# Coarse attention and MoE in one kernel: group-pair loads, a fixed list for the lead-in, and v rows used directly in half of the first coarse output

## The chip, the core and the metric

One core of one Trainium2 chip. The metric is the time of one execution in microseconds (us) on the device, as a median over runs. A core has a matrix engine (TensorE, PE in the profile), a vector engine (VectorE, DVE), an activation engine (ScalarE, ACT), a general engine (GpSimd, POOL), a queue engine (SyncE, SP) and 16 DMA engines. All of them run their own list of instructions in order and wait for one another by semaphores. PSUM is the accumulator memory that matrix products are written to.

## What is computed

q, k and v have 4 batches, 8 heads, 576 positions and 64 columns. Attention is the sum of a coarse part (means over groups of 4 positions, 144 groups) and a local part (a band of 7 positions). Its output, as 2304 tokens x 512, goes through a mixture of 8 experts (512 to 1024 to 512) that are all computed and weighted by a gate with 8 normalizing rounds.

```python
q_d = q.reshape(B, H, Sd, factor, D).mean(axis=3)      # the same for k_d, v_d; factor = 4
out_d = sm_attn(q_d, k_d, v_d)
out_up = np.repeat(out_d, factor, axis=2)
mask = np.abs(pos[:, None] - pos[None, :]) < factor
out_local = np.matmul(softmax(where(mask, scale * q @ k.T, -1e9)), v)
x = (out_up + out_local) as tokens x 512
P = exp(logits - logits.max())          # logits = x @ w_gate
for _ in range(8): normalize P over experts, then over tokens
for e in range(E):
    out += P[:, e:e + 1] * (np.maximum(x @ w1[e], 0.0) @ w2[e])
```

## The kernel before

**Tokens and experts.** The groups are cut into six chunks: three of 64 groups (256 tokens) and three of 128 groups (512 tokens). The expert products begin when chunk 0 is ready: experts 0 to 2 are run on chunk 0 alone, in 24 units of one 128-wide slice of the hidden size each, then experts 3 to 6 on chunks 0 and 1, and so on. Each fp32 matrix is split into a high and a low part, and each product is three matmuls (high by high, high by low, low by high). A unit is 12 matmuls `psh` (L1167, 256 columns), ACT's `hh` (L1224), DVE's `hl` (L1227) and 6 matmuls `psy` of 512 columns (L1195 to L1197). Weights come as raw 256 KB tiles `r`; ACT makes `w1h`, `w2h` (L251, later L1287), POOL or DVE `w1l`, `w2l` (L253, later L1310 on POOL and L1306 on DVE).

**Attention.** For each unit of the local part (`l_gen`) DVE and POOL make products (L357), DVE sums them to scores (L381), masks and normalizes them (L396 to L417), DVE and POOL make products with v (L431) and DVE sums them to `lo` (L462). From b = 1 on the coarse part comes from sums written to memory. For the first 64 groups of b = 0 it is made by functions of their own, in the lead-in, in two halves of four heads, hf0 and hf1, from raw rows `dr` which `d_load` brings: `first_k` sums k over its groups with matmuls against an identity (`pssum`, L654) and ACT copies it to `kz` (L660); `first_v` does that for v (`psv`, L676, to `dv`, L681); `first_q` for q (`psq`, L628); `first_d` makes scores (`pss`, L695), maxima on DVE (`nm`, L705), exponentials on ACT (L708), sums (`sm`, L714), transposes (`pst`, L726), copies (`pt`, L736) and the coarse output (`pso`, L747, to `od`, L755). `x_gen` then puts `lo` in order (`psx`, L942), adds `od` (L948) and splits the sum into `xhs` (ACT, L955) and `xls` (DVE, L958). A third piece, `d_gen`, computes coarse rows 64 to 143 of b = 0 (`psd` L781, `qz` L790, `pss` L840, `st` L848, exponentials L852, transposes `psd` L873, `pt` L878); it borrows one PSUM bank, `psd`, that the local part of the next chunk also uses for its scores (L417 writes it, L431 reads it).

**What sets the order.** Every step is written as a generator ("thread") which gives the engine it wants next and an estimated time from which it can run. In the lead-in (until chunk 0 of x is ready) a loop picks the thread with the earliest estimated time. After that a planner, `sched`, picks the step that can start first by its estimated clocks, ties going by a table of ranks (`RANK`). Engines execute in the order in which the planner has written the instructions, so its estimates fix each queue.

Of the kernel before, what the change touches and what calls it, by code (L numbers as in the profile page):

```python
# [20 lines left out]
def attention_moe_kernel(  # L21
# [597 lines left out]
    v_set = {}  # L619
# [22 lines left out]
    def first_k(hf, kz):  # L642

        for p in range(2):
# [4 lines left out]
            rv = raw[0:HK].rearrange("p k h (a d) -> p k h a d", a=R)  # L649
            ps = y_tile([128, 2, HK], "pssum")  # L650
            for kh in range(2):
                for r in range(R):
                    for h in range(2):
                        nc.tensor.matmul(  # L654
                            out=ps[64 * h:64 * h + 64, kh], lhsT=rv[:, kh, h, r, :], rhs=ident[0:HK, 0:HK],
                            start=(r == 0), stop=(r == R - 1),
                        )
# [6 lines left out]
    def first_v(hf):  # L664

        t_sb = ap2.tile([Q1, 2, 4, D], F32, tag="dv", name="dv")
        done = 0.0
        for p in range(2):
            while (0, hf, p, 2) not in d_raw:
                yield None  # L670
            raw, t_raw = d_raw.pop((0, hf, p, 2))
            yield t_raw
            rv = raw[0:HK].rearrange("p k h (a d) -> p (k h) a d", a=R)
            ps = y_tile([HK, 4, D], "psv")
            for r in range(R):
# [3 lines left out]
            t = pe(3.4, t_raw)  # L679
            yield t + HOP  # L680
            nc.scalar.activation(  # L681
                out=t_sb[0:HK, :, 2 * p:2 * p + 2, :], in_=ps.rearrange("p (k h) d -> p k h d", k=2), func=AF.Copy
            )
            done = act(256, t)
        d_sum[0, hf, 2] = (t_sb, done)

    def first_d(hf, qf):

        while not qf_set or hf not in k_set:
# [11 lines left out]
        sme = su2.tile([128, 2, 2], F32, tag="sme", name="sme")  # L701
        sm = su2.tile([128, 2], F32, tag="sm", name="sm")
        pp = su2.tile([128, 2, SD], F32, tag="pp", name="pp")
        nc.vector.memset(sme, EPS)
# [33 lines left out]
        while (0, hf, 2) not in d_sum:  # L738
            yield None
        vs, t_v = d_sum.pop((0, hf, 2))  # L740
        v_set[hf] = vs
        yield max(t, t_v) + HOP
        ps = ps_h.tile([128, 2, Q0], F32, tag="h", name="pso")
        for p in range(2):
            for i in range(2):
                for kh in range(2):
                    nc.tensor.matmul(  # L747
                        out=ps[64 * i:64 * i + 64, p], lhsT=vs[0:HK, kh, 2 * p + i, :], rhs=pt[:, p, kh, i],
                        start=(kh == 0), stop=(kh == 1),
                    )  # L750
        t = pe(1.4, t, t_v)
# [667 lines left out]
    with tc.manual_schedule():  # L1419
# [74 lines left out]
        def first_x(aa):  # L1494
            for a in aa:
                yield from x_gen(0, a)

# [19 lines left out]
        th["x"] = Thread(first_x((0, 1)))  # L1517
        eng = {"l": "dve", "p": "pool"}
# [610 lines left out]
```

## Time and profile before

| | us |
|---|---|
| median of 3 runs | 1657.15 |
| lowest and highest run | 1655.9 and 1658.35 |
| profiled execution | 1658.6 |
| its span in the trace | 1656.8 |
| mean granted TensorE clock in it | 0.984 |

The page gives busy time of each engine over the span. The rows further down are from the timeline (start, duration, what an instruction writes and reads, how many are merged in a row, and in brackets how long the engine had been idle before and what ended that) and from a table of windows (busy time of each engine in a stretch, the clock that was granted to TensorE, where 0.50 is 1.2 GHz and 1.00 is 2.4 GHz, and what the DMA engines moved). fp32 matmuls that are not split leave two records each, so 16 matmuls are 32 records.

### The profile page before, as it was taken

Reading aid. Unit: us, or ns where it says so; the run is one execution under the profiler, and the core shown is the slowest. Engines: PE = TensorE matmul, PEld = TensorE weight load, DVE = VectorE, ACT = ScalarE, POOL = GpSimd, SP = SyncE. Lnnn points to the kernel's source line nnn. Section 1 sums busy time; section 2 is a strip of 40 time slices with the busy share of each in tenths; the row PEclk is TensorE's granted clock in tenths of the full one; section 3 lists DMA queues with packets and bytes.
Section 4 is the critical chain, followed back from the end, with each engine's and each line's share of the span. In section 5 each row is a group of like instructions: output and inputs, shape, how many; then the busy total and the mean of one; then the engine's idle time right before and its main releaser. Section 6 shows DMA issues by size and latency. Waiting matters only on the chain.

```text
span 1656.8 us, 21885 instructions
## 1 busy us (share of the span) xinstructions
PE 1623.1 (98%) x7845; PEld 1341.0 (81%) x7845; DVE 1007.6 (61%) x1244; ACT 639.3 (39%) x1300; POOL 907.0 (55%) x806
## 2 busy tenths in 40 slices
PE   7999999999999999999999999999999999999998
PEld 5878887888887787887888888888888888888887
DVE  6988889955888759477544464444444444444444
ACT  2654554454454343233333243333333333333331
POOL 5787645586566464566544266444444444444441
PEclk6899999999999999999999999999999999999999
DMA  9689666676664355434221233111111111111112
GB/s 196 168 220 213 176 150 166 161 211 188 167 162 148 114 183 168 139 115 135 76 60 55 95 113 91 52 53 54 53 51 51 51 51 51 51 52 51 52 38 51
DMA packets 201833, 183.68 MB, mean 111 GB/s; under 512 B 23676, under 2 KB 150780, under 8 KB 201468
## 3 DMA queue, kind: packets, MB, share of 16 engines
q1 hardware_dynamic: 194011, 168.65, 37.8%
q10 hardware_dynamic: 7712, 13.64, 2.6%
q8 instruction: 61, 1.00, 0.3%
q14 instruction: 49, 0.39, 0.1%
HBM read 161.66 MB, written 20.58 MB: 110 GB/s over the span
## 4 chain that ended last, share of the span: by engine, by line
PE 88%; DVE 6%; DMA 3%; issue 1%; ACT 1%; POOL 1%; SPq 0%; ACTq 0%; POOLq 0%; DVEq 0%
PE psm L1908 25%; PE psh L1167 15%; PE psy L1988 9%; PE psy L1989 9%; PE psy L1990 9%; PE psy L1195 5%; PE psy L1197 5%; PE psy L1196 5%; PE psh L1388 1%; DVE lo L462 1%; DMA r<-in_moe_w_dram 1%; DVE bsum L1698 1%; DVE prod L431 1%; PE pss L840 1%; DVE tl L1698 1%
## 5 line engine op out<-in xcount | busy, mean ns | idle before, releaser
L1765 POOL TENSOR_TENSOR w2l<-r,w2h 128x512 fp32r<-128x512 f32 x88 | 113.9, 1294 | 377.9 <-ACT w2h L1764 373.9
L1664 DVE SCALAR_TENSOR_TENSOR acc<-psy,lg,acc 128x512 f32<-128x512 f32 x176 | 131.4, 750 | 251.1 <-PE psy L1990 247.5
L1310 POOL TENSOR_TENSOR w1l<-r,w1h 128x512 fp32r<-128x512 f32 x128 | 170.9, 1335 | 159.4 <-ACT w1h L1287 137.3
L1731 POOL TENSOR_TENSOR c1l<-r,c1h 128x512 fp32r<-128x512 f32 (+1 forms) x176 | 206.0, 1196 | 51.7 <-ACT c1h L1728 51.0
L1310 POOL TENSOR_TENSOR w2l<-r,w2h 128x512 fp32r<-128x512 f32 x132 | 179.4, 1360 | 46.0 <-ACT w2h L1287 39.5
L1728 ACT ACTIVATE c1h<-r 128x512 fp32r<-128x512 f32 (+1 forms) x176 | 89.2, 567 | 242.5 <-POOL r L1736 242.5
L1195 PE MATMUL psy<-w2h,hh 128*128 128x512 f32 x416 | 169.1, 406 | 1.8 <-ACT sp L1263 1.6
L1197 PE MATMUL psy<-w2h,hl 128*128 128x512 f32 x416 | 163.5, 393 | 1.8 <-DVE hl L1227 1.8
L1196 PE MATMUL psy<-w2l,hh 128*128 128x512 f32 x416 | 163.5, 393 | 0.0
L1990 PE MATMUL psy<-w2h,xl 128*128 128x512 f32 x400 | 155.6, 389 | 0.0
L1227 DVE SCALAR_TENSOR_TENSOR hl<-psh,hh 128x512 fp32r<-128x512 f32 (+1 forms) x136 | 76.3, 561 | 102.6 <-ACT hh L1224 102.2
L1908 PE MATMUL psm<-tl,c1h 128*128 128x512 f32 x352 | 137.9, 392 | 0.0
L1908 PE MATMUL psm<-th,c1l 128*128 128x512 f32 x352 | 137.9, 392 | 0.0
L1908 PE MATMUL psm<-th,c1h 128*128 128x512 f32 x352 | 137.9, 392 | 0.0
L1988 PE MATMUL psy<-w2h,xh 128*128 128x512 f32 x352 | 136.9, 389 | 0.0
L1989 PE MATMUL psy<-w2l,xh 128*128 128x512 f32 x352 | 136.9, 389 | 0.0
L1167 PE MATMUL psh<-xhs,w1l 128*128 128x256 f32 (+1 forms) x384 | 123.9, 323 | 4.0 <-DVE w1l L1306 4.0
L1167 PE MATMUL psh<-xhs,w1h 128*128 128x256 f32 (+1 forms) x384 | 126.7, 330 | 0.0
L1224 ACT ACTIVATE hh<-psh 128x512 fp32r<-128x512 f32 (+1 forms) x136 | 67.2, 494 | 152.9 <-PE psh L1167 152.5
L1167 PE MATMUL psh<-xls,w1h 128*128 128x256 f32 (+1 forms) x384 | 123.5, 322 | 0.0
L462 DVE TENSOR_REDUCE lo<-prod 128x256 f32<-128x1792 f32 x36 | 121.8, 3392 | 0.3
L1988 PE MATMUL psy<-w2h,xhs 128*128 128x512 f32 x304 | 118.5, 390 | 0.6 <-DVE acc L1664 0.6
(221 smaller groups left out, 3862.1 us busy)
## 6 DMA issues: line engine op xcount, KB each, us to landing
r<-in_moe_w_dram SPq DMA_DIRECT2D x464, 256.0 KB
spill<-sp ACTq DMA_DIRECT2D x42, 256.0 KB
s<-spill SPq DMA_DIRECT2D x42, 256.0 KB
sums<-dr SPq DMA_DIRECT2D x36, 64.0 KB
out_dram<-acc ACTq DMA_DIRECT2D x16, 128.0 KB
lw<-in_k_dram SPq DMA_DIRECT2D x5, 336.0 KB
lw<-in_v_dram SPq DMA_DIRECT2D x5, 336.0 KB
lw<-in_v_dram SPq DMA_DIRECT2D x7, 224.0 KB
```

Of the source, the lines that this page charges most:

```text
L462: nc.vector.tensor_reduce(out=ot[:, :, h % 2], in_=pr.rearrange("p r w d -> p r d w"), axis=AX.X, op=ALU.add,)
L1167: nc.tensor.matmul(out=ps, lhsT=w[:, kk], rhs=x[:, kk], start=(kk == 0 and j == 0), stop=(kk == 3 and j == 2),)
L1195: nc.tensor.matmul(out=ye[z], lhsT=hh[:, ts], rhs=h2, start=(f2 == 0), stop=False)
L1196: nc.tensor.matmul(out=ye[z], lhsT=hh[:, ts], rhs=l2, start=False, stop=False)
L1197: nc.tensor.matmul(out=ye[z], lhsT=hl[:, ts], rhs=h2, start=False, stop=(f2 == NF - 1))
L1310: nc.gpsimd.tensor_tensor(out=l, in0=r, in1=h.bitcast(F32), op=ALU.subtract)
L1664: nc.vector.scalar_tensor_tensor(out=a, in0=y, scalar=g, in1=a, op0=ALU.mult, op1=ALU.add)
L1731: nc.gpsimd.tensor_tensor(out=ls[i][:, s], in0=r[:, s], in1=hs[i][:, s].bitcast(F32), op=ALU.subtract)
L1908: nc.tensor.matmul(out=ps, lhsT=wt[:, kk], rhs=xt[:, kk], start=start and j == 0, stop=j == len(seq) - 1, skip_group_check=not start,)
L1988: nc.tensor.matmul(out=y, lhsT=at_t(h), rhs=h2, start=(f == 0), stop=False)
L1989: nc.tensor.matmul(out=y, lhsT=at_t(h), rhs=l2, start=False, stop=False)
L1990: nc.tensor.matmul(out=y, lhsT=at_t(l), rhs=h2, start=False, stop=(f == 3))
```

## The change

**Loads.** The first k and v rows are read with two neighbouring groups in one partition (64 and 8 partitions x 2 heads x 512 values) where it was one group per partition in two halves (72 partitions x 2 heads x 256 values). The number of DMAs (8 for k, 8 for v) and the bytes are the same; the views in `first_k` and `first_v` follow.

**v rows directly.** For hf1 the group sums of v are no longer made ahead of the coarse output. `pso` sums over the raw rows instead: 32 matmuls from `dr` in place of 8 from `dv`. The summed v that `d_gen` needs later is made by four DVE reductions, after the coarse output is done. Two of four `psv` groups (8 of 16 matmuls) and two of four ACT copies go.

**Order.** The loop of the lead-in gives way to a list, `steps`. x of chunk 0 is two threads, x0 and x1, and `d_gen` starts within the lead-in. The memsets of `sme` stand first. In `sched` a short DVE step which has waited over 2 us for the port shared with POOL gets a better rank.

PE's instructions in the lead-in, up to the first coarse scores of the remaining rows and the first expert product: before,

```order
L628 MATMUL psq<-ident,lq 64x128 x16
L654 MATMUL pssum<-ident,dr 64x72 x64
L695 MATMUL pss<-kz_107,qf 128x144 x2
L676 MATMUL psv<-dr,ident 72x256 x4
L695 MATMUL pss<-kz_108,qf 128x144 x2
L676 MATMUL psv<-dr,ident 72x256 x8
L726 MATMUL pst<-ident,pp 72x128 x4
L676 MATMUL psv<-dr,ident 72x256 x4
L726 MATMUL pst<-ident,pp 72x128 x4
L747 MATMUL pso<-pt,dv 64x64 x16
L942 MATMUL psx<-ident,lo 128x4x32 x8
L781 MATMUL psd<-ident,dr 64x80 x16
```

and after (kz_107 is of hf0, kz_108 of hf1; L651 is `pssum`, L706 and L855 are `pss`, L684 is `psv`, L735 `pst`, L762 `pso`, L957 `psx`, L796 `psd`):

```order
L651 MATMUL pssum<-ident,dr 64x72 x32
L706 MATMUL pss<-kz_107,qf 128x144 x2
L651 MATMUL pssum<-ident,dr 64x72 x32
L706 MATMUL pss<-kz_108,qf 128x144 x2
L735 MATMUL pst<-ident,pp 72x128 x4
L684 MATMUL psv<-dr,ident 72x256 x8
L735 MATMUL pst<-ident,pp 72x128 x4
L762 MATMUL pso<-pt,dv 64x64 x8
L762 MATMUL pso<-pt,dr 64x64 x32
L957 MATMUL psx<-ident,lo 128x4x32 x4
L796 MATMUL psd<-ident,dr 64x80 x16
L957 MATMUL psx<-ident,lo 128x4x32 x4
```

The scores of hf0 moved between the two halves of `pssum`, half of `psv` left, and `psd` moved ahead of the second half of `psx`. The gate products `psg` (eight, ahead of the first `psh` before) now follow 30 matmuls `psh`.

DVE's instructions in the lead-in, from the second pair of score sums: before,

```order
L704 MEMSET sme 128x4
L705 TENSOR_REDUCE nm<-pss 128x2
L396 SCALAR_TENSOR_TENSOR sc<-sc,mask 128x56 x2
L402 TENSOR_REDUCE mx<-sc 128x16
L403 TENSOR_TENSOR sc<-sc,mx 128x112
L714 TENSOR_REDUCE sm<-sme 128x2
L715 RECIPROCAL sm<-sm 128x2
L413 TENSOR_REDUCE mx<-sc 128x16
```

and after, through to the first row maxima of `d_gen` (L714 is `nm`, L723 `sm`):

```order
L403 TENSOR_TENSOR sc<-sc,mx 128x112
L714 TENSOR_REDUCE nm<-pss 128x2
L413 TENSOR_REDUCE mx<-sc 128x16
L414 TENSOR_SCALAR mx<-mx 128x16
L415 RECIPROCAL mx<-mx 128x16
L417 TENSOR_TENSOR sc<-sc,mx 128x112
L431 TENSOR_TENSOR prod<-lw,sc 128x1792
L723 TENSOR_REDUCE sm<-sme 128x2
L724 RECIPROCAL sm<-sm 128x2
L462 TENSOR_REDUCE lo<-prod 128x4x64 x4
L963 TENSOR_TENSOR psx<-psx,od 128x512 x2
L973 TENSOR_TENSOR xls<-psx,xhs 128x4x128 x2
```

The maxima of hf1 moved behind the mask steps, its sums behind the product. The next rows on DVE are, after:

```order
L676 TENSOR_REDUCE dv<-dr 72x128 x4
L862 MEMSET st 80x6
L863 TENSOR_REDUCE st<-pss 80x2
L875 TENSOR_REDUCE st<-st 80x2
L876 RECIPROCAL st<-st 80x2
```

The four new reductions stand ahead of the maxima `st` of the remaining coarse rows.

DVE later, where the second half of `d_gen` meets the local part of the next chunk on the bank `psd`: before,

```order
L417 TENSOR_TENSOR psd<-sc,mx 128x112
L431 TENSOR_TENSOR prod<-lw,psd 128x1792
L1227 SCALAR_TENSOR_TENSOR hl<-psh,hh 128x256
L847 MEMSET st 80x6
L848 TENSOR_REDUCE st<-pss 80x2
L462 TENSOR_REDUCE lo<-prod 128x4x64
```

and after:

```order
L863 TENSOR_REDUCE st<-pss 80x2
L1242 SCALAR_TENSOR_TENSOR hl<-psh,hh 128x256
L381 TENSOR_REDUCE sc<-prod 128x28
L875 TENSOR_REDUCE st<-st 80x2
L876 RECIPROCAL st<-st 80x2
L1242 SCALAR_TENSOR_TENSOR hl<-psh,hh 128x256
```

in which L396 to L417 and L431 follow further down: the maxima and sums of hf1 are through before the local part writes `psd`.

The diff, cut to its core:

```diff
-                for kh in range(2):
-                    s0 = kh * HK * R
-                    nc.sync.dma_start(
-                        out=t[0:HK, kh],
-                        in_=src[b, h0:h0 + 2, s0:s0 + HK * R, :].rearrange("h (p r) d -> p h (r d)", r=R),
-                    )
+                rows = src[b, h0:h0 + 2].rearrange("h (p r) d -> p h (r d)", r=2 * R)
+                for o in (slice(0, 64), slice(64, HK)):
+                    nc.sync.dma_start(out=t[o].rearrange("p h k c -> p h (k c)"), in_=rows[o])
...
         t_sb = ap2.tile([Q1, 2, 4, D], F32, tag="dv", name="dv")
         done = 0.0
+        if hf:
+            while 1 not in od_f:
+                yield None
...
+            if hf:
+                rv = raw[0:HK].rearrange("p h k (a d) -> p k h d a", a=R)
+                for kh in range(2):
+                    nc.vector.tensor_reduce(
+                        out=t_sb[0:HK, kh, 2 * p:2 * p + 2, :], in_=rv[:, kh], axis=AX.X, op=ALU.add
+                    )
+                    done = dve(512, t_raw)
+                continue
...
+        if hf:
+            vr = [d_raw[0, hf, p, 2][0][0:HK].rearrange("p h k (a d) -> p h k a d", a=R) for p in range(2)]
+            t_v = max(d_raw[0, hf, p, 2][1] for p in range(2))
+            parts = [[(kh, vr[p][:, i, kh, r, :]) for kh in range(2) for r in range(R)] for p in range(2) for i in range(2)]
...
+    PATIENCE = 2.0
...
+                if t.lock and t.eng == "dve" and t.dur <= 2.1 and st - max(t.ready, clk["dve"]) > PATIENCE:
+                    rank = 0.4
...
-        th["x"] = Thread(first_x((0, 1)))
-        eng = {"l": "dve", "p": "pool"}
-        while not x_ok(0):
...
+        th["x0"] = Thread(x_gen(0, 0))
+        th["x1"] = Thread(x_gen(0, 1))
+        th["d"] = Thread(d_all())
+        steps = (
+            "l l l l l q q q q q s0 s0 s0 s0 a s1 s1 a s1 s1 l b a l l l b l a a v0 v0 l b l v0 v0 b b a a l "
+            "b b W l w x0 d d l x0 x1 x1 x0 x1 x0 x1 d W v1 v1 W"
+        )
...
+        for nm in steps.split():
             poke()
...
+            if nm == "W":
                 w_convert()
...
+                th[nm].step()
```

## Rows read from the trace of the kernel before

**Rows 1.** The page, part 1: busy us, share, instructions

```profile
PE 1623.1 (98%) x7845; PEld 1341.0 (81%) x7845; DVE 1007.6 (61%) x1244; ACT 639.3 (39%) x1300; POOL 907.0 (55%) x806
```

**Rows 2.** Timeline, PE, lead-in: start, us, what, [idle before <-releaser]

```profile
15.62 5.07 PE L654 MATMUL pssum<-ident,dr 72*64 72x72 f32 x80 [0.91 <-DMA dr<-in_k_dram]
20.62 1.33 PE L695 MATMUL pss<-kz,qf 128*128 128x144 f32 x4
24.93 3.66 PE L676 MATMUL psv<-dr,ident 72*72 72x256 f32 x8 [2.99 <-DMA dr<-in_v_dram]
...
29.34 7.03 PE L676 MATMUL psv<-dr,ident 72*72 72x256 f32 x16
...
40.43 1.06 PE L726 MATMUL pst<-ident,pp 128*72 128x128 f32 x4
41.42 2.03 PE L747 MATMUL pso<-pt,dv 72*64 72x64 f32 x32
...
47.44 1.11 PE L942 MATMUL psx<-ident,lo 128*128 128x128 f32 x4 [2.93 <-DVE lo L462]
48.48 2.40 PE L781 MATMUL psd<-ident,dr 80*64 80x80 f32 x32
...
52.83 0.41 PE L1167 MATMUL psh<-xhs,w1h 128*128 128x256 f32 x1
...
59.29 0.28 PE L1167 MATMUL psh<-xhs,w1h 128*128 128x256 f32 x1
```

**Rows 3.** Timeline, DVE, lead-in

```profile
21.98 0.46 DVE L705 TENSOR_REDUCE nm<-pss 128x2 f32<-128x288 f32 x1 [4.35 <-PE pss L695]
22.36 2.01 DVE L381 TENSOR_REDUCE sc<-prod 128x28 f32<-128x1792 f32 x1
...
32.45 2.02 DVE L431 TENSOR_TENSOR prod<-lw,sc 128x1792 f32<-128x1792 f32 x1
34.50 12.88 DVE L462 TENSOR_REDUCE lo<-prod 128x256 f32<-128x1792 f32 x4
47.26 0.72 DVE L948 TENSOR_TENSOR psx<-psx,od 128x512 f32<-128x512 f32 x1
48.65 0.69 DVE L958 TENSOR_TENSOR xls<-psx,xhs 128x512 fp32r<-128x512 f32 x1 [0.66 <-ACT xhs L955]
```

**Rows 4.** Timeline, ACT, lead-in: two copies that others wait for

```profile
20.73 0.29 ACT L660 ACTIVATE kz<-pssum 128x144 f32<-128x144 f32 x1 [1.63 <-PE pssum L654]
...
52.03 0.60 ACT L790 ACTIVATE qz<-psd 64x160 f32<-64x160 f32 x2
```

**Rows 5.** Windows: stretch, us, busy us of each engine, granted clock, DMA share, GB/s

```profile
25.00:35.00 10.00, 10.00 (x26) 6.24 (x27) 6.52 (x15) 2.95 (x12) 2.72 (x2) 0.50 1.08 252
45.00:52.80 7.80, 5.22 (x44) 4.00 (x45) 5.64 (x6) 5.29 (x12) 7.80 (x7) 0.50 0.56 163
52.80:135.50 82.70, 78.81 (x544) 69.62 (x543) 70.53 (x84) 47.50 (x116) 62.25 (x54) 0.97 0.80 203
88.90:92.30 3.40, 3.19 (x12) 2.76 (x13) 3.29 (x2) 2.21 (x6) 3.40 (x5) 0.50 0.77 252
125.00:150.00 25.00, 25.00 (x132) 21.48 (x131) 20.51 (x21) 12.16 (x24) 21.07 (x20) 1.00 0.93 231
399.50:406.30 6.80, 6.04 (x22) 5.46 (x23) 4.78 (x6) 0.94 (x2) 1.75 (x2) 0.50 0.69 205
```

**Rows 6.** Timeline, ACT and PE, the waits near 86 us

```profile
85.68 0.30 ACT L878 ACTIVATE pt<-psd 72x160 f32<-72x160 f32 x1 [1.70 <-DVE prod L431]
86.04 0.33 PE L873 MATMUL psd<-ident,pp 80*72 80x80 f32 x2 [1.04 <-ACT pt L878]
89.11 0.80 PE L1195 MATMUL psy<-w2h,hh 128*128 128x512 f32 x1 [1.61 <-ACT sp L1263]
```

**Rows 7.** Timeline, DVE and PE, the wait near 396 us

```profile
395.39 3.29 DVE L462 TENSOR_REDUCE lo<-prod 128x256 f32<-128x1792 f32 x1
400.26 0.58 PE L1167 MATMUL psh<-xhs,w1l 128*128 128x256 f32 x1 [4.05 <-DVE w1l L1306]
```

More of the change, by code (lines that the diff above doesn't have):

```diff
@@ L648, in first_k @@
             yield t_raw
-            rv = raw[0:HK].rearrange("p k h (a d) -> p k h a d", a=R)
+            rv = raw[0:HK].rearrange("p h k (a d) -> p h k a d", a=R)
             ps = y_tile([128, 2, HK], "pssum")
@@ L678, in first_v @@
                 )
-            t = pe(3.4, t_raw)
+            t = pe(3.7, t_raw)
             yield t + HOP
             nc.scalar.activation(
-                out=t_sb[0:HK, :, 2 * p:2 * p + 2, :], in_=ps.rearrange("p (k h) d -> p k h d", k=2), func=AF.Copy
+                out=t_sb[0:HK, :, 2 * p:2 * p + 2, :], in_=ps.rearrange("p (h k) d -> p k h d", k=2), func=AF.Copy
             )
             done = act(256, t)
-        d_sum[0, hf, 2] = (t_sb, done)
+        v_set[hf] = t_sb
+        v_t[hf] = done
     def first_d(hf, qf):
+        sme = su2.tile([128, 2, 2], F32, tag="sme", name="sme")
+        nc.vector.memset(sme, EPS)
         while not qf_set or hf not in k_set:
@@ L737, in first_d @@
         t = act(512, t)
[L738 to L741, printed above, removed]
+        if hf:
+            vr = [d_raw[0, hf, p, 2][0][0:HK].rearrange("p h k (a d) -> p h k a d", a=R) for p in range(2)]
+            t_v = max(d_raw[0, hf, p, 2][1] for p in range(2))
+            parts = [[(kh, vr[p][:, i, kh, r, :]) for kh in range(2) for r in range(R)] for p in range(2) for i in range(2)]
+        else:
+            while hf not in v_set:
+                yield None
+            vs, t_v = v_set[hf], v_t[hf]
+            parts = [[(kh, vs[0:HK, kh, z, :]) for kh in range(2)] for z in range(4)]
         yield max(t, t_v) + HOP
@@ L745, in first_d @@
             for i in range(2):
-                for kh in range(2):
+                seq = parts[2 * p + i]
+                for j, (kh, vv) in enumerate(seq):
                     nc.tensor.matmul(
-                        out=ps[64 * i:64 * i + 64, p], lhsT=vs[0:HK, kh, 2 * p + i, :], rhs=pt[:, p, kh, i],
-                        start=(kh == 0), stop=(kh == 1),
+                        out=ps[64 * i:64 * i + 64, p], lhsT=vv, rhs=pt[:, p, kh, i],
+                        start=(j == 0), stop=(j == len(seq) - 1),
                     )
-        t = pe(1.4, t, t_v)
+        t = pe(0.13 * len(parts) * len(parts[0]), t, t_v)
         yield t + HOP
@@ L1491, in attention_moe_kernel @@
         clk["pool"] = 3.0
-        def first_x(aa):
-            for a in aa:
-                yield from x_gen(0, a)
         def first_w():
@@ L1516, in attention_moe_kernel @@
         th["b"] = Thread(first_d(1, qf))
-        th["x"] = Thread(first_x((0, 1)))
-        eng = {"l": "dve", "p": "pool"}
-        while not x_ok(0):
-            poke()
-            cand = []
-            for nm, t in th.items():
-                if t.done or t.ready is None:
-                    continue
-                r = t.ready
-                if nm in eng:
-                    r = max(r, clk[eng[nm]] - 0.3)
-                if nm == "x" and (0, 3) not in l_done:
-                    r += 4
-                if nm == "l" and (0, 3) in l_done:
-                    r = max(r, clk["dve"]) + 50.0
-                cand.append((r, nm))
-            r, nm = min(cand)
-            v_done = (0, 1, 2) in d_sum or 1 in v_set
-            if n_cv[0] < 3 and (v_done or n_cv[0] < 2) and max(w_raw[n_cv[0]][3], clk["act"], clk["pool"] - 1.0) <= r:
+        th["x0"] = Thread(x_gen(0, 0))
[5 more added lines that the diff above has]
+        )
+        for nm, t in list(th.items()):
+            if nm != "d":
+                t.step()
+        for nm in steps.split():
+            poke()
+            if nm == "W":
                 w_convert()
-                continue
-            th[nm].step()
-        while n_cv[0] < 3:
-            w_convert()
+            else:
+                assert th[nm].ready is not None and not th[nm].done, nm
+                th[nm].step()
+        poke()
         now = max(clk["dve"], clk["act"], clk["pool"])
```

15 lines of the change are left out of this document (6 added, 9 removed).

## The prediction, made before the changed kernel was run

> **What bounds the kernel now.** The page comes first: PE is busy 98% of the span, the others 39% to 61% [rows 1]. The change leaves the expert products as they are, so a gain can only come from time in which PE has no expert product to run (the lead-in), waits, or runs at the half clock. The timelines then tell where that time is: expert products begin at 52.83 us [rows 2].
>
> In the lead-in two chains alternate. DVE waits 4.35 us for the scores of hf0, because these stand behind all four sums of k on PE [rows 2, 3]. So its local product starts only at 32.45, and the four sums `lo` behind that run without a gap to 47.4 [rows 3]. PE waits 2.93 us for them, then does `psx`, `psd` and the gate [rows 2]. DVE's chain thus ends last, with PE close behind it, and ACT's copies (`kz`, `qz`) stand between them [rows 4].
>
> Behind the lead-in, PE's longest waits close to what the change moves are at 86 to 92 us and at 396 to 406 us, each with a stretch at half the clock behind it [rows 5 to 7].
>
> **Part 1: DVE's chain starts earlier.** The last 80 records of `pssum` take 5.07 us, 63 ns each, so one tile (32 records) takes 2.03 [rows 2]. The second tile's last 16 records therefore end at 15.62 + 1.01 = 16.63. With hf0's scores moved there, two matmuls of about 0.53 each (four records in 1.33, less the tail) [rows 2], the maxima can start at about 17.9 instead of 21.98: 4.1 us earlier. Then follow: 0.46, a score sum of 2.01 [rows 3], some 0.6 of waiting (hf0's exponentials stand behind the 0.29 us copy of hf1's first k tile on ACT [rows 4], whose sum ends only at about 19.8), the sums and the second score sum to 23.2, the mask steps, and hf1's maxima at 24.0, for which the scores are there (third and fourth tile to 21.8, copy, scores: 22.7). The product starts at about 25.5 instead of 32.45. With 2.0 for it, 0.35 for hf1's sums that now stand behind it, and 12.88 for the four `lo` [rows 3], DVE is through at 40.7 instead of 47.3.
>
> **Part 2: PE becomes the second end of the lead-in.** v lands at 24.93 [rows 2]; I take that as unchanged, since as many DMAs move as many bytes. From there PE has in a row: less the 0.1 to 0.2 by which a step's tail lies under the next: hf0's `psv` 6.83 (16 records in 7.03), `pst` 0.99, `pso` from `dv` half of 1.97, `pso` from raw rows 64 records at 63 ns (2.03 for 32) = 4.0, half of `psx` 1.05, `psd` 2.33, the other half 1.1 [rows 2]. Sum 17.3: PE ends at 42.2, later than DVE's 40.7. The direct use of v thus removes 6.8 of `psv` and adds 4.0 - 1.0 = 3.0 of `pso`, and both count now. After 42.2: addition 0.72, `xhs` 0.66 [rows 3], `qz` 0.60 behind it on ACT [rows 4], scores 0.53, so the first expert product comes at about 44.8 instead of 52.83. The bounds: with PE never late it is DVE's 40.7 and the same tail, 43.5; with v 2 us later it is 46.8.
>
> **Part 3: what is given back.** Not all of those 8 us is gained. The gate's eight matmuls, 2 us ahead of the first product before, only move behind: 0.95 at full clock. In before the clock is 0.50 up to 52.8, and its mean of 0.97 over the next 82.7 us leaves some 5 us at half clock, of which 3.4 lie at 88.9 [rows 5]: it rose about 2 us behind the first `psh`. That is shorter than what now stands ahead of PE's next wait, 18 `psh`, but not by much; I take all 18 at 1.2 GHz, 256 columns in 0.213, to 48.6. There PE needs the scores' PSUM tile, which is free only after maxima on DVE and exponentials on ACT, and these maxima stand behind the four new reductions of v. No row has that reduction. Nearest is `lo`, with strided reads: 12.88 for 4 x 1792 elements, 1.8 ns per element, 0.92 for 512; the other side is the score sum, 2.01 for 1792, 0.57 [rows 3]. The reads here are strided too, so I take 0.92: 3.7 in all against 2.3, and a stall of about 1 us. The first two units' products (24 `psh`, 6 `psy`), which end at 59.29 in before [rows 2], then end at 53.2 to 54.4 by how soon the clock rises, plus 0.95 for the gate. Net gain of the lead-in: 3.9 to 5.1, I take **4.5**. Bounds: 1, with k and v later by 2 to 3 us and a longer stall, and 7, with DVE's bound of 43.5 and an early clock.
>
> The Trainium skill, page "VectorE: DVE Perf Modes", the perf-mode tier table and its rules for kernel authors, speaks against the new reductions: it has `tensor_reduce` at one element per cycle only and advises to restructure it away from a hot path. At its 0.96 GHz an estimate by that page is 0.53 us each, 2.1 in all, under which the stall of 1 us would not come; no row here shows this operation.
>
> **Part 4: the waits at 84 to 92 us.** ACT's `pt` waits 1.70 us for the local part's product L431, because both use the bank `psd`; PE waits 1.04 for `pt` and then 1.61 at `psy`, and its clock is 0.50 for the next 3.4 us, which costs half of that [rows 5, 6]: 4.4 in all. In the new order hf1's coarse maxima and sums are through before the local part writes that bank, so I take all **4.4** as gained; what comes late next there is nothing that I can name. Bounds 0 and 4.4.
>
> **Part 5: the wait at 396 us.** PE waits 4.05 us for a `w1l` which stands on DVE behind a `lo` of 3.29; then the clock is 0.50 for 6.8 us, about 3 us lost [rows 5, 7]. The change names none of this; but the planner works from shifted clocks, writes one `w1l` fewer to DVE, and has low parts of weights ready two units ahead throughout. A plan is an estimate, so I count half: **3.5**, bounds 0 and 7.
>
> **Part 6: what is new.** New waits come from the same shifts. The first 24 units, experts 0 to 2 on chunk 0, end at 135.5; they moved 203 GB/s x 82.7 us = 16.8 MB [rows 5]. They must now have 1.3 MB more (7.8 us at 163 GB/s, which had landed before the start) in about 81 us: 222 GB/s. Stretches with 231 and 252 GB/s are there [rows 5], so it fits, with less slack. I put **3** on new waits, bounds 0 and 8 (one like that of 396 us).
>
> **Sum.** -4.5 - 4.4 - 3.5 + 3.0 = -9.4. The profiled execution of 1658.6 (span 1656.8 and 1.8 around it) stands 1.45 above the median of 1657.15, within the 1655.9 to 1658.35 of the runs and a little beyond; the change is counted off the median: 1657.15 - 9.4 = **1647.7**; a profile like that of before would have a span near 1647.4.
>
> **The rivals.** B, more: both waits go, nothing new comes but 2 us, and the lead-in gains 6.5: -6.5 - 4.4 - 7.2 + 2 = -16.1, **1641**. For it: every wait named has left the new order. Against it: a queue is rewritten over its whole length.
>
> C, less: the lead-in gains its 4.5, but the 7.9 of the two waits comes back at other places, since weights are needed earlier by DVE and POOL, which have as much work as before: **1652.7**. For it: 62.25 of 82.7 us busy on POOL, 70.53 on DVE [rows 5].
>
> D, another clock: if the longer unbroken work of PE raises the clock in the lead-in, PE's 17.3 halve, DVE's 40.7 sets the end (first product at 43.5), and the 18 `psh` cost half of 0.213 each. That is 1.3 + 1.9 better than forecast: **1644.5**. Against it stands 25 to 35 us: PE busy 10.00 of 10.00 us, granted clock 0.50 [rows 5]. The Trainium skill, "TensorE: Matmul & The Clock Gate", Part 1, has it that sustained work raises the clock to 2.4 GHz; by that rule the clock would have risen there, and it did not.
>
> E, slower: the DMA engines become the bound of the first 24 units. They need 18.1 MB after 44.8. At 203 GB/s that takes 89 us and nearly all of the gain goes; below about 197 the change loses. At 190, between the 163 and the 203 of these rows, it takes 95.3 and ends at 140.1, 4.6 after before's 135.5; with one stretch at half clock (3) and the 3.5 of part 5, +4.1: **1661.3**. Against it: 252 GB/s between 25 and 35 us, and a DMA share of 0.80 at 203 [rows 5].
>
> F, it doesn't do what it says: the two-group rows land 2 to 3 us later (64 partitions carry nearly all of a tile instead of 72), or the fixed list waits at a step that the loop would have passed. The lead-in then gains 1 instead of 4.5, and the rest is as in C: **1656.2**.
>
> **Chances.** The forecast, 1644 to 1652: 0.50. B 0.18, C 0.17, D 0.05, E 0.05, F 0.05. The likeliest gives the predicted time. The range reaches into B and over C: 1640.5 to 1655, leaving out half of B, all of E and F. About 0.2% (3.3 us) is what a measurement of this kernel can tell from no change. Faster than 1653.8: the forecast, B, D and half of C, 0.81. Within: the rest of C and F, 0.14. Slower than 1660.5: 0.05.
>
> **What would show it.** Part 1: DVE's wait of 4.35 for `pss` is gone, product L431 starts near 25.5, the last `lo` ends near 40.7. Part 2: first `psh` at 43.5 to 46.5, `psx` of the second half no longer waits for DVE. Part 3: the granted clock stays at 0.50 to about 48 us or later; the four reductions on DVE take 2.3 to 3.7 together; a wait of about 1 us at the second `pss`. Parts 4 and 5: no wait of over 1 us at those places and no half clock behind one. Part 6: the end of unit 24 near 127 us. It is wrong if the first `psh` is later than 48 us, if long waits of PE for weights come up between 45 and 130 us, or if the rest of the span, where nothing was meant to change, differs by several us.

## The result and the profile after

The changed kernel takes 1644.26 us (median of 4 runs, 1644.1 to 1645.82), beside 1657.75 for the kernel before in the same series: a ratio of 0.9918 with an interval of 0.9898 to 0.9937. The forecast was 1647.7, range 1640.5 to 1655. So the direction and the range held; the gain was 13.5 us where 9.4 was forecast. The experiments below show that this agreement is partly luck: one part of the change that the prediction gave no cost at all turned out to decide most of it.

PE's line of the page after answers [rows 1]. The span is 1642.6 us, 14.2 shorter, with the same matmuls:

```profile
PE 1621.2 (99%) x7877; PEld 1341.6 (82%) x7877; DVE 1012.6 (62%) x1247; ACT 638.7 (39%) x1298; POOL 908.9 (55%) x807
```

The lead-in on PE, timeline of the kernel after (start, us, what, idle before and its end), to be read beside [rows 2]:

```profile
15.48 1.33 PE L706 MATMUL pss<-kz,qf 128*128 128x144 f32 x4
...
22.82 7.07 PE L684 MATMUL psv<-dr,ident 72*72 72x256 f32 x16
...
31.59 5.93 PE L762 MATMUL pso<-pt,dr 72*64 72x64 f32 x64
37.45 1.12 PE L957 MATMUL psx<-ident,lo 128*128 128x128 f32 x4
38.50 2.40 PE L796 MATMUL psd<-ident,dr 80*64 80x80 f32 x32
40.83 1.12 PE L957 MATMUL psx<-ident,lo 128*128 128x128 f32 x4
43.55 1.25 PE L855 MATMUL pss<-kz,qz 128*80 128x144 f32 x4 [1.60 <-ACT qz L805]
44.42 0.59 PE L1182 MATMUL psh<-xhs,w1h 128*128 128x256 f32 x1
...
49.30 0.72 PE L855 MATMUL pss<-kz,qz 128*80 128x144 f32 x4 [0.98 <-ACT pp L867]
```

The same stretch on DVE, beside [rows 3]:

```profile
17.62 0.45 DVE L714 TENSOR_REDUCE nm<-pss 128x2 f32<-128x288 f32 x1
...
24.64 2.03 DVE L431 TENSOR_TENSOR prod<-lw,sc 128x1792 f32<-128x1792 f32 x1
...
26.85 12.83 DVE L462 TENSOR_REDUCE lo<-prod 128x256 f32<-128x1792 f32 x4
...
41.98 0.70 DVE L963 TENSOR_TENSOR psx<-psx,od 128x512 f32<-128x512 f32 x1 [1.70 <-PE psx L957]
...
43.95 4.06 DVE L676 TENSOR_REDUCE dv<-dr 72x128 f32<-72x512 f32 x4
```

DVE's wait of 4.35 us for the first scores is gone, the four `lo` end 7.7 us earlier, and now DVE waits for PE (1.70 before the second addition) instead of PE for DVE. The first expert product starts at 44.42 instead of 52.83.

A useful account of the rest is the start of the same expert product in both traces. It can be followed at the points where PE goes over to the next set of chunks:

| first product of | before | after | earlier by |
|---|---|---|---|
| experts 0 to 2 on chunk 0 | 52.8 | 44.4 | 8.4 |
| the next experts, on chunks 0 and 1 | 135.5 | 126.1 | 9.4 |
| those that need chunk 3 | 411.9 | 395.6 | 16.3 |
| those that need the last chunk | 611.7 | 594.7 | 17.0 |
| later experts, from 951 | 951.4 | 937.2 | 14.2 |

[rows 6] have no counterpart: PE's longest wait between 80 and 92 us is 0.35. 6.9 us are gained between the second and the third row of the table, the stretch in which the wait of [rows 7] was: the kernel after has no wait of PE of 0.3 us or more between 333 and 506 us. 2.8 are given back behind 750. There PE waits for DVE, which adds up outputs that had been spilled (timeline of the kernel after, DVE and PE):

```profile
757.81 1.73 DVE L1671 SCALAR_TENSOR_TENSOR acc<-s,lg,acc 128x512 f32<-128x512 f32 x1 [3.08 <-DMA s<-spill]
...
760.26 0.50 PE L1995 MATMUL psy<-w2h,xhs 128*128 128x512 f32 x1 [2.00 <-DVE acc L1671]
```

### The profile page after: what moved, and what is told of

Its sections match the earlier page's. It is cut to its first block, busy times and chain, and to the rows that moved or that the text cites. A ratio compares the mean times of both kernels' runs of the same rounds, so it can differ in the third digit from the quotient of the medians.

```text
span 1642.6 us, 21951 instructions
## 1 busy us (share of the span) xinstructions
PE 1621.2 (99%) x7877; PEld 1341.6 (82%) x7877; DVE 1012.6 (62%) x1247; ACT 638.7 (39%) x1298; POOL 908.9 (55%) x807
## 4 chain that ended last, share of the span: by engine, by line
PE 90%; DVE 3%; DMA 2%; POOL 2%; issue 1%; ACT 1%; SPq 0%; ACTq 0%; POOLq 0%; DVEq 0%
PE psm L1915 26%; PE psh L1182 14%; PE psy L1995 10%; PE psy L1996 10%; PE psy L1997 10%; PE psy L1210 5%; PE psy L1212 5%; PE psy L1211 5%; DMA r<-in_moe_w_dram 1%; PE psh L1406 1%; POOL w1l L1325 1%; POOL w2l L1325 1%; PE pss L855 1%; DVE lo L462 1%; DVE tl L1705 1%
## 5 line engine op out<-in xcount | busy, mean ns | idle before, releaser
L1772 POOL TENSOR_TENSOR w2l<-r,w2h 128x512 fp32r<-128x512 f32 x88 | 114.1, 1296 | 380.8 <-ACT w2h L1771 380.8
L1325 POOL TENSOR_TENSOR w1l<-r,w1h 128x512 fp32r<-128x512 f32 x129 | 175.9, 1364 | 140.1 <-ACT w1h L1302 129.7
L1325 POOL TENSOR_TENSOR w2l<-r,w2h 128x512 fp32r<-128x512 f32 x132 | 175.8, 1332 | 40.6 <-ACT w2h L1302 35.5
```

What stands on the lines that cost most here:

```text
L1325: nc.gpsimd.tensor_tensor(out=l, in0=r, in1=h.bitcast(F32), op=ALU.subtract)
```

## The experiments

Three theories were to be told apart. The first is that of the prediction: the earlier lead-in and the coarse steps that no longer collide with the local part make the gain, and the wait near 396 us goes by a shift in the plan. The second: the planner's new rank, `PATIENCE`, which the prediction left out of its sum, makes it. The third, on the parts of the lead-in: the loads, the list or the direct use of v carries it. All ratios are against the kernel before, run on the same chip in the same series.

| kernel | list | early coarse steps | rank | direct v | pair loads | median us | ratio | interval |
|---|---|---|---|---|---|---|---|---|
| changed kernel again | x | x | x | x | x | 1643.54 | 0.9917 | 0.9903 to 0.9930 |
| half loads | x | x | x | x | | 1645.1 | 0.9929 | 0.9916 to 0.9941 |
| v summed on PE | x | x | x | | x | 1644.38 | 0.9914 | 0.9897 to 0.9930 |
| no early coarse steps | x | | x | x | x | 1647.89 | 0.9934 | 0.9920 to 0.9949 |
| loop instead of the list | | | x | x | x | 1653.49 | 0.9971 | 0.9961 to 0.9981 |
| rank alone, on the kernel before | | | x | | | 1651.78 | 0.9956 | 0.9941 to 0.9971 |
| no rank | x | x | | x | x | 1700.66 | 1.0261 | 1.0240 to 1.0282 |
| no rank, no early coarse steps | x | | | x | x | 1656.94 | 0.9993 | 0.9984 to 1.0003 |

### The changed kernel again, and its loads alone

> The changed kernel itself, as the base for the others of this group. Both theories: 1644 to 1646 us, 12 to 14 below the kernel before, first expert product at 44.4 us, four v reductions 4.1 us together.

The changed kernel took 1643.54 in this series, half a microsecond below what was expected; its first expert product stands at 45.28 in this profile, 0.9 later than in the first. Then its loads:

> Only the first k and v loads go back to two halves with one group per partition; all engines keep exactly the same order of instructions. Theory L (the pair rows land earlier, and PE's part of the lead-in starts with them): the first v sums start near 24.9 us instead of 22.8, the first expert product comes near 46.5 instead of 44.4, and the time is 1646.4, 2.1 above the changed kernel. Rival (the landing is covered, only the new order counts): first product at 44.4, within 0.5 us of the changed kernel.

```diff
-                rows = src[b, h0:h0 + 2].rearrange("h (p r) d -> p h (r d)", r=2 * R)
-                for o in (slice(0, 64), slice(64, HK)):
-                    nc.sync.dma_start(out=t[o].rearrange("p h k c -> p h (k c)"), in_=rows[o])
+                for kh in range(2):
+                    s0 = kh * HK * R
+                    nc.sync.dma_start(
+                        out=t[0:HK, :, kh],
+                        in_=src[b, h0:h0 + 2, s0:s0 + HK * R, :].rearrange("h (p r) d -> p h (r d)", r=R),
+                    )
```

PE's first row of `psv`, of the changed kernel in this series and of the one with half loads:

```profile
23.68 7.07 PE L684 MATMUL psv<-dr,ident 72*72 72x256 f32 x16 [0.90 <-DMA dr<-in_v_dram]
```

```profile
23.82 7.07 PE L687 MATMUL psv<-dr,ident 72*72 72x256 f32 x16 [1.97 <-DMA dr<-in_v_dram]
```

In these two profiles v lands at nearly the same time by either form, the first products stand at 45.28 and 45.42, and the spans are 1643.0 and 1643.1. So the 2.1 us of theory L are not there in them. But the medians are 1.6 us apart, with intervals that overlap, and over all the profiles the first `psv` starts at 23.8 to 25.2 in the three kernels with half loads (this one, the kernel before, and it with the rank) and at 22.3 to 24.4 in the eleven of kernels with pair loads. An effect of the loads of up to some 1.6 us is neither shown nor excluded.

### The coarse output with alternating halves

> In the coarse output over raw v rows the 8 matmuls of one head are no longer in a row: matmuls for the two heads, which write the two halves of the PSUM partitions, alternate. Nothing else moves. Theory H (93 ns instead of 63 ns per record comes from consecutive matmuls into the same half): the 64 records take 4.0 instead of 5.9 us, PE then waits for the last local sum near 39.7, the first product comes 1.1 earlier, near 43.3, and the time is 1.1 us below the changed kernel, 1643.2. Rival (the raw rows as weights are slow by themselves): 5.9 us, same time as the changed kernel.

```diff
-            for i in range(2):
-                seq = parts[2 * p + i]
-                for j, (kh, vv) in enumerate(seq):
+            n_j = len(parts[2 * p])
+            for j in range(n_j):
+                for i in range(2):
+                    kh, vv = parts[2 * p + i][j]
```

PE's timeline of this kernel:

```profile
32.52 3.63 PE L763 MATMUL pso<-pt,dr 72*64 72x64 f32 x64
...
43.18 0.59 PE L1183 MATMUL psh<-xhs,w1h 128*128 128x256 f32 x1
```

64 records take 3.63 us, 57 ns each, where they took 5.93, 93 ns each, with eight matmuls in a row into one half of the PSUM partitions. Theory H holds, and more than forecast: 2.3 us less. The time is 1642.8, a ratio of 0.9911 (0.9898 to 0.9925), 0.7 us below the changed kernel in the same series, which alone would be within the scatter. Of the 2.1 us by which the first product is earlier in these two profiles (43.18 against 45.28), 0.7 are left at the first product of the next experts (126.03 against 126.76).

### The planner's rank taken out

> Only the planner's new rank for DVE steps that wait for the shared port is taken out. Theory P (that rank removed the wait of 4 us at 396 us): a wait of 3 us or more of PE for low weights comes back between 100 and 500 us with a stretch at half clock, 4 to 7 us above the changed kernel, 1648 to 1651. Theory S (the shifted start alone changed the plan there): within 2 us of the changed kernel, 1642 to 1646.

```diff
-    PATIENCE = 2.0
+    PATIENCE = 1e9
```

1700.66 us: not 4 to 7 us above the changed kernel, but 57, and 43 above the kernel before. Neither theory had this size. Of this kernel, the rows of PE and DVE where its two largest losses arise:

```profile
132.27 1.09 PE L957 MATMUL psx<-ident,lo 128*128 128x128 f32 x4 [5.68 <-DVE lo L462]
135.48 0.80 PE L1182 MATMUL psh<-xhs,w1h 128*128 128x512 f32 x1 [2.12 <-ACT xhs L970]
136.63 0.68 DVE L973 TENSOR_TENSOR xls<-psx,xhs 128x512 fp32r<-128x512 f32 x1
...
429.01 2.02 DVE L431 TENSOR_TENSOR prod<-lw,psd 128x1792 f32<-128x1792 f32 x1
...
431.08 2.24 PE L915 MATMUL psd<-pt,dv 72*64 72x144 f32 x16 [11.33 <-DVE prod L431]
...
443.66 0.68 DVE L973 TENSOR_TENSOR xl<-psx,xh 128x512 fp32r<-128x512 f32 x1
444.28 0.78 PE L1182 MATMUL psh<-xh,w1h 128*128 128x512 f32 x1
```

And the rows that answer them in the kernel after:

```profile
113.04 0.69 DVE L973 TENSOR_TENSOR xls<-psx,xhs 128x512 fp32r<-128x512 f32 x1 [0.60 <-ACT xhs L970]
...
126.07 0.39 PE L1182 MATMUL psh<-xhs,w1h 128*128 128x512 f32 x1
...
382.97 0.69 DVE L973 TENSOR_TENSOR xl<-psx,xh 128x512 fp32r<-128x512 f32 x1 [0.72 <-ACT xh L970]
...
395.63 0.39 PE L1182 MATMUL psh<-xh,w1h 128*128 128x512 f32 x1
```

L973 is the last step of x of a chunk. With the rank, this step starts 13.0 us before PE needs chunk 1 and 12.7 before it needs chunk 3. Without it, PE waits 5.68 us for the last `lo` of chunk 1, 2.12 for `xhs` and 1.09 for `xls`. For chunk 3 it waits 11.33 us for the bank `psd`, which the local part's late product L431 holds, then 3.67 and 4.00 more. So in this kernel the local part falls behind without the rank, and PE runs into it. That does not hold of every kernel without the rank: in the kernel before, the last L958 of chunk 3 starts at 357.23, 54.7 us before PE needs it at 411.92.

### The rank alone, and the lead-in without it

> The kernel before, with only the planner's new rank for DVE steps that wait for the shared port added. First expert product near 52.8 us as before. Theory P1 (the rank is a gain of its own: it takes away the waits that low weights and late products cause): the wait of 4 us at 396 us and its half clock go, the waits at 84 to 92 us stay, time 1648 to 1651. Theory P2 (the rank only cures what the earlier start brings about; the kernel before kept pace without it): within 2 us of the kernel before.

```diff
+    PATIENCE = 2.0
...
+                if t.lock and t.eng == "dve" and t.dur <= 2.1 and st - max(t.ready, clk["dve"]) > PATIENCE:
+                    rank = 0.4
```

> The changed kernel without the three early coarse steps in the list and without the planner's new rank. Theory F (with the earlier start the plan needs the rank; local products of the next chunks fall behind weight conversions without it, whatever the list does with the coarse steps): chunk 1 or 3 of x is ready later than PE needs it, PE waits 4 us or more for it, 1665 to 1700. Theory G (only the early coarse steps bring the loss without the rank): the kernel without early coarse steps plus the 6 to 7 us that the rank was worth on the kernel before, 1652 to 1657.

```diff
-    PATIENCE = 2.0
+    PATIENCE = 1e9
...
-            "b b W l w x0 d d l x0 x1 x1 x0 x1 x0 x1 d W v1 v1 W"
+            "b b W l w x0 l x0 x1 x1 x0 x1 x0 x1 W v1 v1 W"
...
         th["x"] = Thread(x_all())
+        th["d"] = Thread(d_all())
         th["w"] = Thread(w_gen())
```

The rank alone brings the kernel before to 1651.78, ratio 0.9956: theory P1, 0.8 above the range that it gave. The list, the loads and the direct use of v without the rank and without the early coarse steps bring nothing that the interval tells from no change: 1656.94, ratio 0.9993, although PE's first product comes at 47.0 instead of 52.8. That is theory G. The place is the wait of [rows 7]. In the kernel with the lead-in but no rank it is there as before, DVE's `w1l` behind a `lo`:

```profile
391.94 3.29 DVE L462 TENSOR_REDUCE lo<-prod 128x256 f32<-128x1792 f32 x1
395.16 1.60 DVE L1321 TENSOR_TENSOR w1l<-r,w1h 128x512 fp32r<-128x512 f32 x1
...
396.82 0.43 PE L1182 MATMUL psh<-xhs,w1l 128*128 128x256 f32 x1 [4.05 <-DVE w1l L1321]
```

In the kernel before with the rank, one `w1l` has gone ahead of that `lo`:

```profile
391.60 0.98 DVE L1306 TENSOR_TENSOR w1l<-r,w1h 128x512 fp32r<-128x512 f32 x1
392.50 3.38 DVE L462 TENSOR_REDUCE lo<-prod 128x256 f32<-128x1792 f32 x1
396.13 0.68 DVE L1306 TENSOR_TENSOR w1l<-r,w1h 128x512 fp32r<-128x512 f32 x1
...
396.86 0.39 PE L1167 MATMUL psh<-xhs,w1l 128*128 128x256 f32 x1 [1.15 <-DVE w1l L1306]
```

Where the rank is missing the wait is 4.05 us, to the hundredth that of the kernel before; where it is added, 1.15. It is 1.15 too in the two kernels with the rank and without the early coarse steps, of which one starts the expert products at 46.60 and the other, with the loop, at 53.28. So the wait at 396 us is cut by the rank, and an earlier start does not move it. With rank and early coarse steps together, in the changed kernel, nothing of it is left. By the start of the same expert products the rank alone costs 1.6 us up to 135 us, gains 4.1 from there to 412, and 3.5 behind that.

### The early coarse steps

> The changed kernel, in whose list only the three steps that begin coarse rows 64 to 143 are taken out; they then run under the planner, as in the kernel before. Theory C (the early start keeps the coarse steps of hf1 clear of the local part's use of the same PSUM bank): waits of 1 us or more on PE for the copy pt or behind it, between 70 and 95 us, with a stretch at half clock, are back: 4 us, and the gate is ahead of the first product again (46 us): 1648 to 1651. Rival (the collision does not return, since the planner's rank or the earlier start moves it): 1644 to 1646.

The diff is that of the list above, with the rank left in. ACT and PE of this kernel, beside [rows 6]:

```profile
81.76 0.30 ACT L893 ACTIVATE pt<-psd 72x160 f32<-72x160 f32 x1 [1.70 <-DVE prod L431]
82.11 0.34 PE L888 MATMUL psd<-ident,pp 80*72 80x80 f32 x2 [1.03 <-ACT pt L893]
...
85.19 0.50 PE L1210 MATMUL psy<-w2h,hh 128*128 128x512 f32 x1 [1.63 <-ACT sp L1278]
```

They are the three waits of before, 1.70, 1.04 and 1.61, moved 4 us. Theory C holds: the early start of `d_gen` in the list is what removes them. The time is 1647.89, ratio 0.9934 against 0.9917: about 2.8 us (0.17% of 1658), somewhat less than the 4 forecast and at the edge of what the intervals tell apart. The traces show why it is not more. At the first product of the next experts the changed kernel is 5.6 us ahead of this one (126.76 against 132.33), and near 700 us, at the same psy, 6.7 (683.41 against 690.06). Behind 750 us the changed kernel waits 2.0 us for a spilled output and this one does not, and 2.8 are left at the end.

Without the rank the same early steps are harmful: 1700.66 with them, 1656.94 without. Where that loss arises is shown above; why the early steps bring it about when the rank is missing was not tried and stays open.

### The list against the loop

> The changed kernel with the loop of the kernel before in place of the fixed list (the four v reductions only after chunk 0 of x, coarse rows 64 to 143 not begun in the lead-in); loads, direct v rows and the planner's rank stay. Theory O (the order that the list sets is most of the lead-in's gain): hf0's maxima wait on DVE for all four k sums again, first expert product at 50 to 52 us, the waits near 85 us are back, 1650 to 1655. Rival (loads, direct v and the rank carry it): within 3 us of the changed kernel, under 1647.

```diff
-        for nm in steps.split():
+        while not x_ok(0) or not th["v1"].done:
             poke()
+            cand = []
...
+            r, nm = min(cand)
```

DVE and PE of this kernel:

```profile
20.94 0.46 DVE L714 TENSOR_REDUCE nm<-pss 128x2 f32<-128x288 f32 x1 [3.13 <-PE pss L706]
28.26 0.46 DVE L714 TENSOR_REDUCE nm<-pss 128x2 f32<-128x288 f32 x1 [2.76 <-PE pss L706]
...
46.09 1.11 PE L957 MATMUL psx<-ident,lo 128*128 128x128 f32 x4 [5.64 <-DVE lo L462]
...
53.28 0.58 PE L1182 MATMUL psh<-xhs,w1h 128*128 128x256 f32 x1
```

Theory O: both waits of DVE for `pss` are there, PE waits 5.64 for the last `lo`, and the first product is at 53.28, no earlier than before. Direct v and the loads alone shorten PE's part, which was not the bound. The time, 1653.49, is no better than with the rank alone.

### v summed on PE

> The changed kernel with hf1's v summed on PE again (16 psv matmuls in all, coarse output from the sums, no v reductions on DVE); list, loads and rank stay. By the steps of the prediction PE's chain has 6.9 us of psv more and 4.9 of pso less than measured after, so the first product comes at about 46.5 to 47.5 instead of 44.4 to 45.3, the wait of 1 to 1.8 us at the second coarse scores goes: +1 to +2, 1645 to 1646. Rival (DVE's chain sets the end anyway): same as the changed kernel. Rival (the planner's later course turns with it): 3 us or more to either side behind 100 us.

```diff
-        if hf:
-            vr = [d_raw[0, hf, p, 2][0][0:HK].rearrange("p h k (a d) -> p h k a d", a=R) for p in range(2)]
...
+        while hf not in v_set:
+            yield None
+        vs, t_v = v_set[hf], v_t[hf]
...
-            "b b W l w x0 d d l x0 x1 x1 x0 x1 x0 x1 d W v1 v1 W"
+            "b b W l w x0 d d l x0 x1 x1 x0 x1 x0 x1 d W W"
```

PE of this kernel:

```profile
47.69 1.25 PE L839 MATMUL pss<-kz,qz 128*80 128x144 f32 x4 [1.60 <-ACT qz L789]
48.56 0.59 PE L1166 MATMUL psh<-xhs,w1h 128*128 128x256 f32 x1
```

The first product is 3.3 us later than in the changed kernel of the other series (45.28), and a microsecond later than expected; v landed at 24.4 here. The same psy stand 2.4 us later until 700 us, and then that difference is gone: the wait behind 750 us does not arise here, and the time is 1644.38, ratio 0.9914, as with the direct use, and not the 1 to 2 us longer that were expected. So the direct use of v does what it should in the lead-in, and its gain ends in the wait for spilled outputs.

### The additions of spilled outputs

> The changed kernel; of the four additions of spilled outputs that DVE makes ahead of the first four psy sums of the later experts, the last is moved behind them. Three buffers hold spilled tiles, so the fourth must wait for a load that starts only when the first is used. Theory W (in the changed kernel PE's wait of 2.2 us at 758 us, with the half clock behind it, comes from that fourth addition, which takes back 2.7 us of what was gained by 700 us): the wait is gone, 2 to 2.8 us below the changed kernel, 1641 to 1642. Rival (psy would wait for DVE there anyway): no difference, 1643.5 to 1644.3.

```diff
                     if pl is accp:
                         back_add()
-                        back_add()
+                        if f == 0:
+                            back_add()
...
                     if pl is accp:
                         back_add()
+                        if t == 3:
+                            back_add()
```

DVE of this kernel at that place:

```profile
750.60 4.12 DVE L1671 SCALAR_TENSOR_TENSOR acc<-s,lg,acc 128x512 f32<-128x512 f32 x3
754.63 0.74 DVE L1671 SCALAR_TENSOR_TENSOR acc<-psy,lg,acc 128x512 f32<-128x512 f32 x1
758.30 1.25 DVE L1671 SCALAR_TENSOR_TENSOR acc<-s,lg,acc 128x512 f32<-128x512 f32 x1 [2.93 <-DMA s<-spill]
```

DVE still waits 2.93 us for the fourth load, but the addition of `psy`, which PE waits for, now stands ahead of it, and PE's wait is gone. 1640.13 us, ratio 0.9889 (0.9875 to 0.9904): by the ratios 4 to 5 us below the changed kernel, 3.9 by the start of the same psy in the two traces. Theory W, with more than it forecast.

> The same, and the coarse output over raw v rows with alternating halves, as in the run that alternates them. If both effects add: 0.3 to 0.8 below the one before, 1640.5 to 1641.5. Rival (an earlier start is lost again in later waits): the same as with the later addition alone.

The diff is the sum of the two. 1639.09 us, ratio 0.9883 (0.9867 to 0.9900): the fastest of all, 18.6 us below the kernel before in its series. It stands 1.0 below the later addition alone. PE of this kernel:

```profile
39.44 1.11 PE L958 MATMUL psx<-ident,lo 128*128 128x128 f32 x4 [1.01 <-DVE lo L462]
...
43.03 0.59 PE L1183 MATMUL psh<-xhs,w1h 128*128 128x256 f32 x1
```

PE waits for DVE's last `lo` again, 1.01 us; both chains of the lead-in now end nearly together.

### One more step in the list

> The same as the one before, and the list begins the first coarse maxima of rows 64 to 143 ahead of the four v reductions on DVE. By the steps: PE's wait of 1 to 1.8 us at the second coarse scores goes, 1639.5 to 1640.5. Since the planner starts from other clocks, its whole order behind the lead-in is another; if that counts for more than the lead-in does, the result lies 3 us or more off this value, to either side, by waits behind 60 us.

```diff
-            "b b W l w x0 d d l x0 x1 x1 x0 x1 x0 x1 d W v1 v1 W"
+            "b b W l w x0 d d l x0 x1 x1 x0 x1 x0 x1 d W r0 r0 r0 v1 v1 W"
```

1680.36 us, ratio 1.0134 (1.0115 to 1.0152): 41 us slower than the kernel that it differs from by three steps. The first expert product is at 43.2 us, as early as there. The loss arises behind it. Its first large wait, on ACT and PE:

```profile
88.65 0.63 ACT L1303 ACTIVATE w2h<-r 128x512 fp32r<-128x512 f32 x1 [7.97 <-DMA r<-in_moe_w_dram]
...
90.40 0.80 PE L1211 MATMUL psy<-w2h,hh 128*128 128x512 f32 x1 [5.03 <-ACT hh L1240]
```

ACT stands 7.97 us at a weight that has not landed, and ACT's `hh`, which PE needs, is queued behind it. Further waits of PE follow (2.95 us at 181 us, 2.90 at 319, 2.37 at 358, 2.57 at 419). By the start of the same psy the loss grows until about 550 us and then stays. The planner had other clocks to start from and wrote another order; which step of it costs what was not tried. With the rank taken out this is the second case in which the order behind the lead-in is worth tens of us, the lead-in itself a few.

## Why the prediction was right or wrong

**Parts 1 and 2, the lead-in: right, with two errors that cancel.** DVE's maxima came at 17.62 (forecast 17.9), the product at 24.64 (25.5), the last `lo` ended at 39.7 (40.7), PE's chain at 41.95 (42.2), and the first product at 44.42 (44.8, bounds 43.5 to 46.8). The 0.6 us of waiting that part 1 put before the sums on DVE did not occur. Two terms of PE's chain were off. v was there before 22.8, not at 24.93; it differs from run to run by more than a microsecond, and whether the change of loads has a part in it stays open. And `pso` over raw rows took 5.93, not 4.0: the 2.03 for 32 records of `pso` in [rows 2] came from matmuls that change the half of the PSUM partitions after every second one, the new ones do so after every eighth, 93 ns; alternating they take 57. The lower bound of 43.5 has too short a tail: it puts 2.8 us between the last `lo` and the first product, in which the second half of `psx`, which needs that `lo`, has no place. Where PE did wait for the last `lo`, in the fastest kernel, that `lo` ended at 39.39 and the product came 3.64 later, so DVE's 40.7 would have given 44.3; D leans on the same bound.

**Part 3, what is given back: right, a little too much.** The reductions took 4.06 in all (3.7 taken, 2.3 to 3.7 given as bounds: the upper bound was too low by a tenth), the stall at the second scores was 0.98 (1 forecast). The 24 `psh` and 6 `psy` end at 52.45, and the gate's 0.94 is still to come: 5.9 us ahead of 59.29, where 4.5 was taken, 3.9 to 5.1 computed; in the second profile of the same kernel they end at 53.32, which makes it 5.0. The clock rose after 15 `psh`, not after 18: their spacing falls from 0.213 to 0.12 at 47.8 us. (The clock column of that profile shows 1.00 over the whole lead-in, which these spacings contradict; I go by the spacings.) That the clock in before is 0.50 up to 52.8 holds only from about 15 us on; between 7.5 and 15 its mean is 0.92. The Trainium skill, "VectorE: DVE Perf Modes", perf-mode tier table, has `tensor_reduce` at the lowest rate only, from which the prediction's estimate was 0.53 us for one such reduction. Measured is 1.01, near the 0.92 from the strided `lo`, and the stall that this estimate excluded came; the measurement decides.

**But the lead-in's gain is not worth its size at the end.** The sum counts what PE gains at 53 us as gained at 1657, and only the 3 us of part 6, which were looked for in the first 128 us, stand against it. In the kernel with the early lead-in but neither rank nor early coarse steps the same psy stand 5.8 us ahead at 57 us, 3.4 at 150, 4.7 at 700 and 2.0 at 990, and the time is that of before (0.9993). The wait behind 750 us, 2 us on PE and some half clock, takes part of what arrives there early.

**Part 4, the waits at 84 to 92 us: right in mechanism.** They are gone, and they come back as they were when the early coarse steps are taken out of the list; in time that was 2.8 us at the end, not 4.4. At the first product of the next experts the early steps were worth 5.6, with what they gain in the lead-in itself, and behind 750 us part of that was lost again, as said above.

**Part 5, the wait at 396 us: the step that failed.** "The change names none of this" was wrong. The change names it in the three lines of the rank, which the diff shows and the prediction does not cost. Half of 7 was taken for a shift of the plan. What the runs show in its place: the wait stands unmoved where the lead-in is earlier and the rank is missing (4.05 us), and shrinks to 1.15 where the rank is added to the kernel before. The rank is worth 6.6 us on the kernel before, and 57 in the changed kernel. The sum came out near because the rank happened to bring what a shift was credited with. By the table of starts, the lead-in and the waits at 84 to 92 us gave 9.4 where 4.5 + 4.4 were forecast, and the stretch with the wait at 396 us gave 6.9 where 3.5 was: most of the miss lies in the term whose cause was wrong.

**Part 6, new waits: about right, in another place.** 3 us were put on them. They came as 2.8 us behind 750 us, where the prediction did not look; the first 24 units end at 126.1, forecast 127, and rival E's shortage of transfers did not come (the kernel after moved 214 GB/s between 48 and 128 us, and PE waited for weights there 0.6 us at most).

**The rivals.** B came half true: both waits went, but 2.8 us came back behind 750. C and F did not come. D's time, 1644.5, is nearly the measured one, but its mechanism did not occur: the clock did not rise in PE's chain behind the landing of v, which it was to halve. It was up before that. With half loads it was 1.00 from 15 to 20 us, but PE then only waited longer for v (1.97 us), and from 24 us on PE was busy 18.00 of 18.00 us at 0.50 (windows of that kernel, columns as [rows 5]):

```profile
15.00:20.00 5.00, 4.00 (x71) 3.10 (x70) 4.97 (x5) 1.41 (x6) 4.47 (x1) 1.00 0.94 173
24.00:42.00 18.00, 18.00 (x137) 13.95 (x137) 16.05 (x10) 4.98 (x14) 13.85 (x6) 0.50 1.07 230
```

The slower end, which the prediction put on transfers with 0.05, was real by a mechanism that it did not name: without the rank the same lead-in loses 43 us.

## What to carry to other kernels

Where a planner sets the order, a line that changes its ranks has to be costed like a moved instruction: ask which queue it lets past which, and who waits there; here three such lines were worth more than the rewritten lead-in without its early coarse steps, and three more steps in a list cost 41 us. A gain at the start counts only as far as the next wait that does not move with it, so follow the same instruction through both traces at several places before adding it to the sum. And a kernel that is faster by a new order of a long plan should be judged by taking its parts out one at a time, since each part's worth depends on the others.

## What the runs showed of the hardware

At the half clock, fp32 matmuls of 64 columns and 72 rows took 93 ns per record with eight in a row into the same 64 PSUM partitions, and 57 ns when two halves alternated. The reduction of 4 strided values into one over 512 elements took 1.01 us, 1.98 ns per element, where the contiguous score sum takes 1.12 (2.01 for 1792) [rows 3]. With the loop in place of the list the clock did rise within the lead-in, at about 34 us (two windows of that kernel):

```profile
28.00:34.00 6.00, 6.00 (x33) 3.91 (x32) 5.46 (x13) 3.81 (x12) 3.03 (x2) 0.52 1.13 278
34.00:40.00 6.00, 3.64 (x74) 3.51 (x70) 6.00 (x3) 2.63 (x6) 6.00 (x3) 1.00 1.08 175
```

The Trainium skill, "TensorE: Matmul & The Clock Gate", Part 1, ties the clock to sustained work of PE; the 18 us of full work at 0.50 above do not agree with that, and what decided between these two cases is open.
